# Bucketed attention and a GELU layer on one core: the first batch's softmax division moved behind the value product

## The chip, the core and the metric

One core of a Trainium2 chip. The metric is the device time of one execution in microseconds, lower is better; the median of several executions is compared. TensorE (PE) multiplies and also turns tiles; VectorE (DVE), ScalarE (ACT) and GpSimd (POOL) work element by element; SyncE (SP) issues the transfers.

## What is computed

```python
mask = q_bucket[:, :, :, None] == k_bucket[:, :, None, :]
scores = scale * np.matmul(q, k.transpose(0, 1, 3, 2))
scores = np.where(mask, scores, -1000000000.0)
scores = scores - np.max(scores, axis=-1, keepdims=True)
attn = np.exp(scores)
attn = attn / (np.sum(attn, axis=-1, keepdims=True) + 1e-09)
attn_out = np.matmul(attn, v)
x = attn_out.transpose(0, 2, 1, 3).reshape(B * S, H * D)
h = x @ w_in
out = 0.5 * h * (1.0 + erf(h / np.sqrt(2.0))) @ w_out
```

There are 4 batches, 8 heads, 768 positions and 64 features of a head; the bucket of a position is a number of 6 signs of a projection; the layer is 512 wide with 2048 hidden features. All inputs are float32.

## The kernel before

The work of the attention comes in units: one head and 128 queries against all 768 keys, 48 units in a batch, 192 in all. Two heads make a pair; 256 queries are a chunk, so a pair and a chunk take four units. For a unit (`unit`, L750), PE makes the scores with four matmuls (L765, ring `s` of 2 PSUM buffers), DVE finds the largest of each row (L768) and a small product of it (L772), ACT takes the exponentials into ring `p` (L778; 2 buffers in the first batch, a third later) and sums each row on the way. The sum gets 1e-9 added (`total`, on ACT, DVE or POOL) and DVE takes its reciprocal (L787).

From there the batches differ (`WHOLE`, L26). In batch 0 everything stays in float32: `whole_turn` (L824) multiplies the exponentials by the reciprocal in place (`divided`: 128x768 on ACT, DVE or POOL), PE turns them in six 128x128 transposes (L833) into two PSUM buffers of the ring `hp`, and two copies (ACT or DVE) bring them into the ring `pt`. `values` (L865) multiplies the turned tiles of a pair and chunk with the values (L880, 24 matmul records), and two steps bring the result into `x` in two float16 parts: ACT writes the high part with the scale of the values (L907), DVE the low part (L914). In the batches 1 to 3 the exponentials are divided and split into two float16 parts and turned by DMA; the change leaves these as they are.

Beside the units of batch 0 the same engines make the operands of each head (`head`: rounding, low parts, moves by an engine or by a DMA of SP, three projection matmuls, signs) and decode and split the weights (`weight_pair`, above all DVE: L486, L491, L496, L529, L555). The layer (L1074, ACT's gelu, L1122, L1141) follows chunk by chunk. Its first group of hidden features waits for the last score matmuls of batch 0 (`early_steps`), because its buffers lie where the fourth set of head operands lay.

All steps are listed first, each with engines it may run on, an estimated cost, a due time (the unit's number less or plus one of the numbers of `PAR`) and the steps it needs. `Plan.order` plays them through once, picks for each free engine the ready step that is due first, and so fixes the engine of each step and the order of each queue. On the chip every engine then works through its queue in that order; an instruction that waits holds everything queued behind it on its engine.

Of the kernel before, what the change touches and what calls it, by code (L numbers as in the profile page):

```python
# [32 lines left out]
PAR = dict(DR_ACT=180.03, DR_DVE=32.78, SI0=-234.76, SI1=321.18, SI2=-274.91, SI_ACT=-435.45, SI_DVE=-244.85, SI_Pool=-136.99, Z=598.64, VS0=-117.63, H0=565.92, HL=-600, VS=-594.8, G2=600, HQ=446.27, VQ=519.55, in0=341.87, out0=361.65, in1=54.07, out1=512.39, in2=153.92, out2=299.76, in3=338.81, out3=348.44, H1=487.41, H2=501.77, H3=-314.52, H4=53.2, H5=190.41, H6=-565.9, H7=135.72, MEV=-462.42, MGE=592.79, MSP=572.47, V0=-392.16, QK0=142.58, QK1=-179.17, QK2=174.11, MX0=-38.24, MX1=-334.15, MX2=-600, EX0=59.88, EX1=-101.95, EX2=460.15, NR0=94.12, NR1=-587.27, NR2=19.84, HI0=374.58, HI1=-275.4, HI2=-597.26, LO0=-600, LO1=-438.84, LO2=388.37, PV0=159.29, PV1=-533.03, PV2=-322.05, TR0=-526.38, TR1=-567.47, TR2=-42.11, V1=463.52, V2=314.42, Sin0=-61.75, Sin1=512.25, Sin2=326.03, Sin3=-253.09, Sout0=383.99, Sout1=-516, Sout2=360.56, Sout3=-232.19, Lin=532.76, Pin=460.34, Qin=600, Cin=-7.38, Min=536.23, Lout=600, Pout=600, Qout=-207.73, Cout=-600, Mout=363.48, G0=167.04, G1=-500.44, G3=146.24, G4=-508.01, G5=-323.28, G6=-126.53, G7=117.72, DUP0=357.52, DUP1=339.32, DUP2=361.88, LOW0=171.54, LOW1=-375.7, LOW2=-591.9, PRJ0=351.84, PRJ1=115.77, PRJ2=594.01, MSK0=404.11, MSK1=383.24, MSK2=187.87, DI_ACT=581.05, DI_DVE=-600, DI_Pool=587.5, WS_ACT=344.23, WS_DVE=401.15, WS_Pool=582.63, WH_ACT=-449.61, WH_DVE=519.61, WH_Pool=151.81, WL_ACT=-261.43, WL_DVE=-196.91, WL_Pool=-597.4, VH_ACT=345.12, VH_DVE=363.9, VH_Pool=-55.33, MV_SP=600, MV_ACT=600, MV_DVE=-499.53, MV_Pool=-197.62, LO_ACT=-128.53, LO_DVE=-14.71, LO_Pool=376.22, RND_ACT=-445.94, RND_DVE=62.58, RND_Pool=405.55, MSK_ACT=-183.07, MSK_DVE=-71.72, MSK_Pool=177.11, HI_ACT=96.96, HI_DVE=423.53, HI_Pool=32.64, DG_ACT=-156.41, DG_DVE=-190.46, DG_Pool=-42.95, EV_ACT=324.28, EV_DVE=41.66, EV_Pool=565.57, GH_ACT=50.45, GH_DVE=14.78, GH_Pool=91.5)  # L33
HOPX = {"PE": -0.03, "DVE": -0.1, "ACT": 0.12, "Pool": 0.27, "SP": 1.04}
BIG = 2.0**34
# [187 lines left out]
def tile_bucket_attention_moe(  # L223
# [33 lines left out]
        "s": 2, "hp": 4, "p": 2, "hl": 2, "raw": 1, "rawe": RAWE, "sign": 1, "pt": NTH + 1,  # L257
        "x": NTH, "vraw": 1, "vhl": 2, "wraw": 3, "o": 2, "diag": 1, "h": 1,
    }
# [3 lines left out]
    def ring(pool, name, shape, dtype, count, first=0):  # L263
# [16 lines left out]
        "vhl": ring(const, "vhl", [P, 2, KT, P], F16, 2),  # L280
        "wraw": [wbits[:, n * 1024 : (n + 1) * 1024] for n in range(rings["wraw"])],
        "o": ring(const, "o", [P, 1024], F32, rings["o"]),
        "diag": ring(const, "diag", [P, P], BF16, 1),
# [3 lines left out]
        for i in range(NSET)  # L287
    ]
    rows = const.tile([P, NT, 5], F32, tag="rows", name="rows")
    tiny = const.tile([P, 4 * NSC + 2 * B, 4], F32, tag="tiny", name="tiny")  # L290
# [15 lines left out]
    for i in range(NSET + 1, NSET + 1 + NEARLY):  # L306
        sets.append([
            early.tile([P, S], F32R, tag=f"{nm}{i}", name=f"{nm}{i}") for nm in ("Aq", "Ak", "Bq", "Bk")
        ])
    bufs["rawe"] = ring(early, "rawe", [P, S], F32, rings["rawe"])  # L310

# [438 lines left out]
    def unit(t, i, qs, cl, whole, made, place):  # L750
# [26 lines left out]
        def exps():  # L777
            nc.scalar.activation(  # L778
                out=buf(ex).rearrange("p (b k) -> p b k", b=2), in_=both(sp), func=AF.Exp, scale=sc, bias=nb,
                accum_out=ssum,  # L780
            )

        def total():
            affine(su.engine, si, ssum, unity, 1e-9 * unity)

# [18 lines left out]

        unity = 1.0 if whole else 2.0**-15
# [7 lines left out]
        if whole:  # L813
            return sp, whole_turn(ex, nr, r, place, cl, t)
        hi = add(affine_on("HI", S, True), 0, high, t + PAR[f"HI{cl}"], [nr], takes="hl", port=True)
# [5 lines left out]
        free(hi, [tr])  # L821
        return sp, [tr]

    def whole_turn(ex, nr, r, place, cl, t):  # L824

        hold, u = place

        def divided():
            affine(dg.engine, buf(ex), buf(ex), r)
# [13 lines left out]

        dg = add(affine_on("DG", S, True), 0, divided, t + PAR[f"HI{cl}"], [nr], port=True)
        if not hold:
            hold.append(add("none", 0, lambda: None, -10, [dg], takes="pt"))
        prods, copies = [], []
        for n, (k0, k1) in enumerate(((0, KT // 2), (KT // 2, KT))):
            step = []
            step.append(  # L850
                add("PE", TURN * (k1 - k0), lambda k0=k0, k1=k1, step=step: product(k0, k1, step), t + PAR[f"LO{cl}"], [dg, hold[0]], takes="hp")
            )
# [12 lines left out]
    def values(b, pr, ch, whole, vhl, turns, holds, key):  # L865

# [39 lines left out]
        def high():  # L906
            nc.scalar.activation(  # L907
                out=buf(xt[b, ch])[:, 0, pr, :nt], in_=buf(parts[0])[:, :nt], func=AF.Copy,
                scale=s_v[:, b : b + 1] if whole else 2.0**-15,
            )  # L910

        def low():
            x = buf(xt[b, ch])
            nc.vector.scalar_tensor_tensor(  # L914
                out=x[:, 1, pr, :nt], in0=buf(parts[0])[:, :nt], scalar=s_v[:, b : b + 1] if whole else 2.0**-15, in1=x[:, 0, pr, :nt],
                op0=ALU.mult, op1=ALU.subtract,
            )

        needs = [parts[-1]]
# [39 lines left out]
    for b in range(B):  # L959
# [3 lines left out]
        for h in range(2 * NPAIR):  # L963
            pr = h // 2
            if h % 2 == 0:
                key, mms = t - PAR[f"V{cl}"], []
                whole = pr < WHOLE[b]
                vhl = values_whole(b, pr, key) if whole else values_halves(b, pr, key, v_ready[b])
                holds, turns = {}, {}
            i = min(range(n_sets), key=lambda i: (used.get(i, -1), i))  # L970
# [4 lines left out]
            for ch in chunks:  # L975
                holds[h % 2, ch], turns[h % 2, ch] = [], []
                for u in range(ch[1] // P):
                    qs = slice(ch[0] + u * P, ch[0] + (u + 1) * P)
                    sp, tr = unit(t, i, qs, cl, whole, made, (holds[h % 2, ch], u))
                    uses.append(sp)  # L980
                    turns[h % 2, ch] += tr
                    t += 1
                if h % 2:
                    mms.append(
                        values(
                            b, pr, ch, whole, vhl, turns[0, ch] + turns[1, ch], [holds[0, ch], holds[1, ch]],
                            t + PAR[f"PV{cl}"],
                        )
                    )
# [238 lines left out]
```

## Time and profile before

| | |
|---|---|
| time, median of 3 runs | 901.4 us (901.18 to 901.84) |
| the profiled execution | 900.17 us, its span 898.1 us |
| PE, DVE, ACT, POOL busy | 95%, 77%, 71%, 25% of the span |
| granted TensorE clock, mean | 0.992 of full speed |

The span runs from the first to the last instruction of the profiled execution; its time has some 2 us around it. A busy time is the time in which at least one record of the engine is open. Records of one engine overlap: an instruction's record opens before the one ahead of it has closed, so what an instruction takes from its queue is the distance from its start to the next start, which is less than the length of its record. The same holds for matmuls more strongly.

### The profile page before, as it was taken

What the parts mean: (1) busy time and instruction counts of PE and PEld (TensorE: products, weight loads), DVE (VectorE), ACT (ScalarE), POOL (GpSimd) and SP (SyncE); (2) the same over time, 40 slices, a digit from 0 to 9 for tenths busy, and PEclk for the clock granted to TensorE, in tenths of its full rate; (3) what the DMA queues carried; (4) which work ended last, traced back from release to release, by engine and by line L of the source; (5) the groups of instructions that cost most, each with busy time, mean ns of one, the idle gap of its engine ahead of it and who ended that gap; (6) DMA issues with size and microseconds to landing.
All of it is one profiled execution on the core that took longest, in us unless ns stands there. A gap on an engine that the chain in (4) does not pass through costs nothing.

```text
span 898.1 us, 17035 instructions
## 1 busy us (share of the span) xinstructions
PE 855.6 (95%) x6452; PEld 610.5 (68%) x6452; DVE 695.3 (77%) x1337; ACT 635.0 (71%) x1050; POOL 225.8 (25%) x239
## 2 busy tenths in 40 slices
PE   4898988979999999999999999999999999999997
PEld 2665666766676777867677667767767767676663
DVE  8899999989999999987997987897897761212112
ACT  5888988786878878877787887887887762232231
POOL 5544534231422422310311323131231110000000
PEclk9899999989999999999999999999999999999999
DMA  8655542454496998875767689779499651000000
GB/s 269 189 180 168 147 133 95 112 124 94 107 161 145 208 211 161 172 152 117 163 150 158 153 165 188 137 143 189 80 195 145 118 111 20 24 1 25 1 24 23
DMA packets 269745, 115.79 MB, mean 129 GB/s; under 512 B 228576, under 2 KB 253152, under 8 KB 269664
## 3 DMA queue, kind: packets, MB, share of 16 engines
q1 hardware_dynamic: 269488, 114.72, 58.5%
q8 instruction: 50, 0.82, 0.4%
q14 instruction: 31, 0.25, 0.1%
q10 hardware_dynamic: 176, 0.00, 0.0%
HBM read 41.95 MB, written 6.29 MB: 54 GB/s over the span
## 4 chain that ended last, share of the span: by engine, by line
PE 75%; DVE 16%; ACT 5%; issue 2%; DMA 1%; SPq 0%; POOL 0%; DVEq 0%; ACTq 0%
PE hp L1141 25%; PE hp L1074 24%; PE s L765 12%; PE hp L889 8%; DVE s L768 4%; ACT p L778 2%; PE hp L880 1%; PE hp L833 1%; DVE Bq L688 1%; PE hp L725 1%; PE hp L727 1%; DVE hl L793 1%; DMA Bk<-Aq 1%; PE hp L726 1%; DVE wbits L793 1%
## 5 line engine op out<-in xcount | busy, mean ns | idle before, releaser
L1074 PE MATMUL hp<-x,Win 128*128 128x256 f16 x2304 | 267.5, 273 | 0.8 <-DVE tiny L529 0.8
L1141 PE MATMUL hp<-Wout,g 128*128 128x512 f16 x1152 | 265.6, 380 | 0.0
L1074 PEld LDWEIGHTS <-Win 128*128 128x128 f16 x2304 | 220.7, 98 | 41.2 <-issue 12.3
L1141 PEld LDWEIGHTS <-g 128*128 128x128 f16 x1152 | 107.1, 98 | 128.4 <-issue 13.3
L768 DVE TENSOR_REDUCE s<-s 128x1 f32<-128x768 f32 x192 | 181.7, 959 | 16.1 <-PE s L765 14.1
L778 ACT ACTIVATE p<-s,rows 128x768 f32<-128x768 f32 x148 | 145.9, 987 | 21.9 <-DVE rows L772 14.1
L765 PE MATMUL s<-Ak,Aq 128*128 128x384 f32 x360 | 141.7, 394 | 11.4 <-ACT p L778 9.5
L1084 ACT ACTIVATE h<-hp,ffs 128x512 f32<-128x512 f32 x96 | 65.2, 683 | 103.3 <-PE hp L1074 102.7
L765 PE MATMUL s<-Bk,Bq 128*128 128x384 f32 x360 | 123.3, 343 | 0.0
L1122 DVE SCALAR_TENSOR_TENSOR g<-h,ffs,g 128x512 f16<-128x512 f32 x96 | 75.2, 796 | 48.2 <-ACT g L394 43.4
L765 PEld LDWEIGHTS s<-Ak,Aq 128*128 128x128 f32 x360 | 69.2, 192 | 36.4 <-ACT p L778 23.1
L397 DVE TENSOR_SCALAR g<-h,ffs 128x512 f16<-128x512 f32 x42 | 21.2, 505 | 75.1 <-PE hp L1141 60.6
L889 PE MATMUL hp<-pt,vhl 128*64 128x256 f16 x1296 | 76.3, 274 | 1.7 <-DVE vhl L650 1.6
L889 PEld LDWEIGHTS <-vhl 128*64 128x64 f16 x1296 | 68.7, 110 | 11.1 <-issue 9.2
L765 PEld LDWEIGHTS s<-Bk,Bq 128*128 128x128 f32 x360 | 69.6, 193 | 1.0
L793 DVE SCALAR_TENSOR_TENSOR wbits<-p,rows,wbits 128x768 f16<-128x768 f32 x56 | 60.0, 1074 | 2.4 <-ACT wbits L394 2.1
L397 POOL TENSOR_SCALAR rows<-rows 128x1 f32<-128x1 f32 x50 | 20.0, 401 | 162.0 <-ACT p L778 89.6
L417 POOL TENSOR_TENSOR Bk<-raw,Aq 64x768 fp32r<-64x768 f32 x24 | 45.6, 1900 | 36.6 <-ACT Aq L394 35.2
L833 PE MATMUL hp<-ident,p 128*128 128x128 f32 x288 | 42.6, 282 | 8.1 <-POOL p L397 2.7
L778 ACT ACTIVATE wbits<-s,rows 128x768 f32<-128x768 f32 x44 | 43.3, 984 | 8.5 <-DVE rows L772 7.1
L793 DVE SCALAR_TENSOR_TENSOR hl<-p,rows,hl 128x768 f16<-128x768 f32 x44 | 45.9, 1051 | 1.0 <-POOL hl L397 0.7
L1108 ACT ACTIVATE h<-h 128x2048 f32<-128x2048 f32 x24 | 45.9, 1911 | 0.4
(164 smaller groups left out, 1167.5 us busy)
## 6 DMA issues: line engine op xcount, KB each, us to landing
raw<-qk SPq DMA_DIRECT2D x28, 384.0 KB, 3.6
vraw<-v SPq DMA_DIRECT2D x28, 384.0 KB, 4.0
wbits<-w_in SPq DMA_DIRECT2D x16, 512.0 KB, 3.7
wbits<-w_out SPq DMA_DIRECT2D x16, 512.0 KB, 4.2
out<-o SPq DMA_DIRECT2D x12, 512.0 KB, 2.8
Bq<-Aq SPq DMA_DIRECT2D x18, 192.0 KB, 2.8
Ak<-Aq SPq DMA_DIRECT2D x17, 192.0 KB, 3.0
Bk<-Aq SPq DMA_DIRECT2D x13, 192.0 KB, 2.9
```

Source lines behind the costliest of these rows:

```text
L417: on.tensor_tensor(out=out, in0=in0, in1=in1, op=ALU.subtract)
L765: nc.tensor.matmul(to, x, y, start=k == 0, stop=k == 1)
L768: nc.vector.tensor_reduce(out=buf(sp)[:, SPARE + 1 : SPARE + 2], in_=both(sp), axis=AX.XY, op=ALU.max, negate=True)
L778: nc.scalar.activation(out=buf(ex).rearrange("p (b k) -> p b k", b=2), in_=both(sp), func=AF.Exp, scale=sc, bias=nb, accum_out=ssum,)
L793: nc.vector.scalar_tensor_tensor(out=buf(hi)[:, 1], in0=buf(ex), scalar=r, in1=buf(hi)[:, 0], op0=ALU.mult, op1=ALU.subtract,)
L833: nc.tensor.transpose(buf(step[0])[:, (k - k0) * P : (k - k0 + 1) * P], buf(ex)[:, words(k)], ident32,)
L889: nc.tensor.matmul(pv[j * D : (j + 1) * D], buf(vh)[:, tv, kt, j * D : (j + 1) * D], buf(holds[j][0])[:, tp * KT + kt, :nt], start=kt == 0 ...
L1074: nc.tensor.matmul(buf(pair[0])[:, j * ch[1] : (j + 1) * ch[1]], win_hl[:, f0 // WB1, tw, pr, f0 % WB1 : f0 % WB1 + P], x[:, tx, pr, : ch[1]],
L1084: nc.scalar.activation(out=bufs["h"][0][:, 2 * fp : 2 * fp + 2, :nt], in_=buf(pair[0])[:, : 2 * nt].rearrange("p (j k) -> p j k", j=2), fu ...
L1108: nc.scalar.activation(out=h, in_=h, func=AF.Gelu)
L1122: nc.vector.scalar_tensor_tensor(out=gt[:, 1, s2, :nt], in0=h[:, s2, :nt], scalar=sg, in1=gt[:, 0, s2, :nt], op0=ALU.mult, op1=ALU.subtract,)
L1141: nc.tensor.matmul(buf(banks[u]), gt[:, tg, f, u * P : (u + 1) * P], wout_hl[:, ft // UT, tw, ft % UT], start=fresh and f == ti == 0, stop ...
```

## The change

In batch 0 the exponentials are no longer divided before they are turned. `whole_turn` needs only the exponentials. Their row sums go to a column each of a new tile `sums`. For each pair and chunk (12 in the batch) a new function `divisors` works on the sums of its four units at once: it adds 1e-9, takes one reciprocal of 128x4, spreads the factors to a tile of 128x256 (each factor 64 times), lets PE turn this with two 128x128 transposes into a buffer of `hp`, and copies it to SBUF (`rb`, 2 buffers). After the value product, DVE multiplies the product by the scale of the values and by these factors (`divided`, in `values`) into `rb`, an engine writes the high float16 part from it and DVE or POOL subtracts for the low part; before, ACT and DVE did the two parts straight from PSUM. The two transposes of `divisors` join `early_steps`, so the layer's first group waits for them too. All due times are other numbers, the planner's estimate of a transpose is 0.11 in place of 0.1 and three of its hop times are others, so the whole order is made anew, that of the later batches too.

```diff
-TURN = 0.1
+TURN = 0.11
...
-HOPX = {"PE": -0.03, "DVE": -0.1, "ACT": 0.12, "Pool": 0.27, "SP": 1.04}
+HOPX = {"PE": -0.03, "DVE": -0.09, "ACT": 0.12, "Pool": 0.01, "SP": 0.82}
...
-                accum_out=ssum,
+                accum_out=sums[:, t : t + 1] if whole else ssum,
...
+        if whole:
+            return sp, whole_turn(ex, place, cl, t), ex
...
-        dg = add(affine_on("DG", S, True), 0, divided, t + PAR[f"HI{cl}"], [nr], port=True)
         if not hold:
-            hold.append(add("none", 0, lambda: None, -10, [dg], takes="pt"))
+            hold.append(add("none", 0, lambda: None, -10, [ex], takes="pt"))
...
+    def divisors(t, cl, exs):
...
+        def spread():
+            for_u = all_of(shares).rearrange("p j u -> p u j").unsqueeze(3)
+            affine(rs.engine, buf(rs), for_u.to_broadcast([P, UT, 2, D]))
+
+        def turn():
+            for u in range(UT):
+                nc.tensor.transpose(
+                    buf(rt)[:, u * P : (u + 1) * P], buf(rs)[:, u].rearrange("p j d -> p (j d)"), ident32
+                )
+
+        def copy():
+            affine(rc.engine, buf(rc), buf(rt)[:, :TC])
+
+        su = add({e: (c, PAR[f"SI_{e}"]) for e, c in (("ACT", 0.23), ("DVE", 0.07), ("Pool", 0.16))}, 0, total, t + PAR["RB"], exs)
+        nr = add("DVE", 0.07, norm, t + PAR["RB"], [su])
+        rs = add(affine_on("RS", TC), 0, spread, t + PAR["RB"], [nr], takes="spread", port=True)
+        rt = add("PE", 2 * TURN, turn, t + PAR["RB"], [rs], takes="hp")
+        free(rs, [rt])
+        early_steps.append(rt)
+        rc = add({e: (c, PAR[f"EV_{e}"]) for e, c in (("ACT", 0.28), ("DVE", 0.34))}, 0, copy, t + PAR["RB"], [rt], takes="rb")
+        free(rt, [rc])
+        return rc
...
+        def divided():
+            nc.vector.scalar_tensor_tensor(
+                out=buf(rc), in0=buf(parts[0])[:, :nt], scalar=s_v[:, b : b + 1], in1=buf(rc),
+                op0=ALU.mult, op1=ALU.mult,
+            )
...
         if whole:
-            needs.append(v_ready[b])
-        hi = add("ACT", 0.06 + 0.21 * nt / TC + 0.093 * whole, high, -10, needs)
-        lo = add("DVE", 0.07 + 0.27 * nt / TC, low, -10, [hi])
-        free(parts[0], [lo])
+            xm = add("DVE", 0.41, divided, -10, [parts[-1], rc, v_ready[b]])
+            free(parts[0], [xm])
+            hi = add(affine_on("XH", TC), 0, high_of, -10, [xm], port=True)
+            lo = add(subtract_on("XL", TC), 0, low_of, -10, [hi], port=True)
+            free(rc, [lo])
```

## Rows read from the trace of the kernel before

**Rows 1.** Windows: stretch, length; PE, PEld, DVE, ACT, POOL busy (records); clock; DMA.

```profile
22.00:166.00 144.00, 129.21 (x905) 92.17 (x906) 138.99 (x322) 125.83 (x253) 65.72 (x69) 0.98 0.51 147
166.00:202.00 36.00, 31.39 (x237) 25.13 (x236) 33.68 (x63) 29.01 (x46) 10.05 (x10) 0.91 0.58 131
202.00:898.00 696.00, 685.59 (x5276) 487.20 (x5274) 503.68 (x924) 468.37 (x736) 137.42 (x141) 1.00 0.60 121
```

**Rows 2.** The same view, two pieces of the first stage.

```profile
22.00:90.00 68.00, 59.33 (x397) 42.12 (x398) 64.66 (x150) 59.06 (x116) 33.16 (x35) 0.96 0.61 180
90.00:108.00 18.00, 17.96 (x123) 12.40 (x122) 17.80 (x43) 16.32 (x36) 8.83 (x9) 1.00 0.40 121
```

**Rows 3.** Chain that ended last, 88:108 (start us, us, what).

```profile
93.18 0.90 PE s L765 x4
94.08 0.66 PE hp L833 x6
94.73 1.01 PE hp L880 x8
...
101.76 0.71 PE s L765 x4
```

**Rows 4.** Lines on PE, 22:166 (count | busy us, mean ns | idle before).

```profile
L833 PE MATMUL hp<-ident,p 128*128 128x128 f32 x284 | 42.1, 282 | 8.1 <-POOL p L397 2.7 <-DVE x L914 1.9 <-DVE rows L772 1.2
```

**Rows 5.** The same view, DVE.

```profile
L768 DVE TENSOR_REDUCE s<-s 128x1 f32<-128x768 f32 x46 | 43.9, 957 | 3.2 <-PE s L765 3.1
L397 DVE TENSOR_SCALAR pt<-hp 128x384 f32<-128x384 f32 x29 | 15.8, 551 | 0.9 <-PE hp L833 0.7
...
L787 DVE RECIPROCAL rows<-rows 128x1 f32<-128x1 f32 x47 | 7.4, 158 | 0.2
...
L914 DVE SCALAR_TENSOR_TENSOR x<-hp,s_v,x 128x256 f16<-128x256 f32 x11 | 5.2, 477 | 0.0
...
L397 DVE TENSOR_SCALAR p<-p,rows 128x768 f32<-128x768 f32 x2 | 1.2, 622 | 0.0
```

**Rows 6.** The same view, ACT.

```profile
L394 ACT ACTIVATE pt<-hp 128x384 f32<-128x384 f32 x65 | 29.6, 486 | 6.8 <-PE hp L833 6.3
L394 ACT ACTIVATE p<-p,rows 128x768 f32<-128x768 f32 x25 | 23.2, 935 | 5.8 <-DVE rows L787 5.6
...
L394 ACT ACTIVATE rows<-rows 128x1 f32<-128x1 f32 x27 | 5.5, 202 | 0.7
L907 ACT ACTIVATE x<-hp,s_v 128x256 f16<-128x256 f32 x11 | 5.1, 465 | 1.5 <-PE hp L880 1.4
```

**Rows 7.** The same view, POOL.

```profile
L397 POOL TENSOR_SCALAR p<-p,rows 128x768 f32<-128x768 f32 x21 | 21.0, 1001 | 38.1 <-DVE rows L787 29.3 <-DVE rows L772 2.6 <-DVE tiny L387 2.5
L417 POOL TENSOR_TENSOR Bk<-raw,Aq 64x768 fp32r<-64x768 f32 x4 | 8.1, 2026 | 5.7 <-ACT Aq L394 5.4
...
L397 POOL TENSOR_SCALAR diag<-ident,tiny 128x128 bf16<-128x128 bf16 x4 | 1.5, 373 | 4.3 <-DVE tiny L529 1.9 <-PE hp L432 0.9 <-DVE inv_v L383 0.9
```

**Rows 8.** DVE, then ACT in order of time (start us, us, instruction).

```profile
71.60 0.16 DVE L787 RECIPROCAL rows<-rows 128x1 f32<-128x1 f32 x1
71.67 0.21 DVE L772 SCALAR_TENSOR_TENSOR rows<-limit,s 128x2 f32<-128x2 f32 x1
...
73.80 0.20 ACT L394 ACTIVATE rows<-rows 128x1 f32<-128x1 f32 x1
73.91 0.47 ACT L394 ACTIVATE pt<-hp 128x384 f32<-128x384 f32 x1
74.28 0.39 ACT L394 ACTIVATE diag<-ident,tiny 128x128 bf16<-128x128 bf16 x1
```

**Rows 9.** What PE waited for, 22:166 (us in total, times, longest us).

```profile
PE hp L833 <- POOL p L397: 2.7, 3, 1.2
```

**Rows 10.** PE, then ACT in order of time, the end of the first batch.

```profile
159.84 1.47 PE L1074 MATMUL hp<-x,Win 128*128 128x256 f16 x12
...
160.71 0.99 ACT L778 ACTIVATE p<-s,rows 128x768 f32<-128x768 f32 x1
```

More of the change, by code (lines that the diff above doesn't have):

```diff
@@ L257, in tile_bucket_attention_moe @@
         "s": 2, "hp": 4, "p": 2, "hl": 2, "raw": 1, "rawe": RAWE, "sign": 1, "pt": NTH + 1,
-        "x": NTH, "vraw": 1, "vhl": 2, "wraw": 3, "o": 2, "diag": 1, "h": 1,
+        "x": NTH, "vraw": 1, "vhl": 2, "wraw": 3, "o": 2, "rb": 2, "spread": 1, "diag": 1, "h": 1,
     }
@@ L288, in tile_bucket_attention_moe @@
     ]
+    n_whole = 2 * KT * WHOLE[0]
+    assert not any(WHOLE[1:])
+    sums = const.tile([P, n_whole + KT], F32, tag="sums", name="sums")
+    shares = const.tile([P, n_whole + KT], F32, tag="shares", name="shares")
     rows = const.tile([P, NT, 5], F32, tag="rows", name="rows")
@@ L309, in tile_bucket_attention_moe @@
         ])
+    bufs["spread"] = ring(early, "spread", [P, UT, 2, D], F32, 1)
     bufs["rawe"] = ring(early, "rawe", [P, S], F32, rings["rawe"])
@@ L821, in unit, with whole_turn @@
         free(hi, [tr])
-        return sp, [tr]
-    def whole_turn(ex, nr, r, place, cl, t):
+        return sp, [tr], ex
+    def whole_turn(ex, place, cl, t):
         hold, u = place
-        def divided():
-            affine(dg.engine, buf(ex), buf(ex), r)
         def product(k0, k1, step):
@@ L850, in whole_turn @@
             step.append(
-                add("PE", TURN * (k1 - k0), lambda k0=k0, k1=k1, step=step: product(k0, k1, step), t + PAR[f"LO{cl}"], [dg, hold[0]], takes="hp")
+                add("PE", TURN * (k1 - k0), lambda k0=k0, k1=k1, step=step: product(k0, k1, step), t + PAR[f"LO{cl}"], [ex, hold[0]], takes="hp")
             )
@@ L863, in whole_turn, with all_of, total, norm @@
         return copies
-    def values(b, pr, ch, whole, vhl, turns, holds, key):
+    def divisors(t, cl, exs):
+        def all_of(tile_):
+            return tile_[:, t : t + 2 * KT].rearrange("p (j k) -> p j k", j=2)[:, :, : UT]
+        def total():
+            affine(su.engine, all_of(sums), all_of(sums), 1.0, 1e-9)
+        def norm():
+            nc.vector.reciprocal(out=all_of(shares), in_=all_of(sums))
+        def spread():
[17 more added lines that the diff above has]
+        return rc
+    def values(b, pr, ch, whole, vhl, turns, holds, key, rc):
         vh, vl = vhl
@@ L907, in high @@
             nc.scalar.activation(
-                out=buf(xt[b, ch])[:, 0, pr, :nt], in_=buf(parts[0])[:, :nt], func=AF.Copy,
-                scale=s_v[:, b : b + 1] if whole else 2.0**-15,
+                out=buf(xt[b, ch])[:, 0, pr, :nt], in_=buf(parts[0])[:, :nt], func=AF.Copy, scale=2.0**-15,
             )
@@ L914, in low, with high_of, low_of @@
             nc.vector.scalar_tensor_tensor(
-                out=x[:, 1, pr, :nt], in0=buf(parts[0])[:, :nt], scalar=s_v[:, b : b + 1] if whole else 2.0**-15, in1=x[:, 0, pr, :nt],
+                out=x[:, 1, pr, :nt], in0=buf(parts[0])[:, :nt], scalar=2.0**-15, in1=x[:, 0, pr, :nt],
                 op0=ALU.mult, op1=ALU.subtract,
             )
-        needs = [parts[-1]]
-        if whole:
-            needs.append(v_ready[b])
-        hi = add("ACT", 0.06 + 0.21 * nt / TC + 0.093 * whole, high, -10, needs)
-        lo = add("DVE", 0.07 + 0.27 * nt / TC, low, -10, [hi])
-        free(parts[0], [lo])
+        def divided():
[3 more added lines that the diff above has]
+            )
+        def high_of():
+            affine(hi.engine, buf(xt[b, ch])[:, 0, pr, :nt], buf(rc))
+        def low_of():
+            x = buf(xt[b, ch])
+            subtract(lo.engine, x[:, 1, pr, :nt], buf(rc), x[:, 0, pr, :nt])
+        if whole:
+            xm = add("DVE", 0.41, divided, -10, [parts[-1], rc, v_ready[b]])
[3 more added lines that the diff above has]
+            free(rc, [lo])
+        else:
+            hi = add("ACT", 0.06 + 0.21 * nt / TC, high, -10, parts[-1:])
+            lo = add("DVE", 0.07 + 0.27 * nt / TC, low, -10, [hi])
+            free(parts[0], [lo])
         x_parts[b, ch] += [hi, lo]
@@ L968, in tile_bucket_attention_moe @@
                 vhl = values_whole(b, pr, key) if whole else values_halves(b, pr, key, v_ready[b])
-                holds, turns = {}, {}
+                holds, turns, exs = {}, {}, []
             i = min(range(n_sets), key=lambda i: (used.get(i, -1), i))
@@ L978, in tile_bucket_attention_moe @@
                     qs = slice(ch[0] + u * P, ch[0] + (u + 1) * P)
-                    sp, tr = unit(t, i, qs, cl, whole, made, (holds[h % 2, ch], u))
+                    sp, tr, ex = unit(t, i, qs, cl, whole, made, (holds[h % 2, ch], u))
                     uses.append(sp)
+                    exs.append(ex)
                     turns[h % 2, ch] += tr
@@ L983, in tile_bucket_attention_moe @@
                 if h % 2:
+                    rc = divisors(t - KT - UT, cl, exs[-KT - UT : -KT] + exs[-UT:]) if whole else None
                     mms.append(
```

10 lines of the change are left out of this document (4 added, 6 removed).

## Prediction

> **What bounds the kernel now.** I read the windows first, to see which engine is full in which stretch. From 202 us on, PE has records open in 685.6 of 696 us at full clock [rows 1]: there the end moves only with PE's work, and the change takes none from it. What can be won lies before. In the stage of the first batch, 22 to 166 us, DVE is open in 139.0 of 144 us (96.5%), ACT in 125.8 (87%), PE in 129.2 and POOL in 65.7 [rows 1]. So DVE is the fullest, with ACT near behind, and the pieces say the same: 64.7 of 68 us up to 90, then 17.8 of 18 [rows 2].
>
> A busy PE is not a full one, so I read the chain next, in the one piece where it runs through PE alone: four score matmuls take 0.71 to 0.90 us, six transposes 0.66, eight matmuls of the value product 1.01 [rows 3]. A unit has four, six and six of these: 0.71 + 0.66 + 0.76 = 2.1 us at the least and 2.3 at the most. The stage holds 46 units [rows 5], 98 to 107 us. They are 184 + 284 + 264 of PE's 905 records (the last: 11 products of 24, as there are 11 of L914) [rows 1, 4, 5]; for the other 173 I estimate 0.11 each as of a transpose, 19 us. PE thus has 117 to 126 us of work in 144. It is the third engine near its limit, but in this stage not the first. The stage ends when the last of three queues is through, and shortening it shortens the whole, since what follows is PE's own work in an unbroken row.
>
> **What an instruction takes from its queue.** Records overlap. On DVE a reciprocal of 0.16 us is followed after 0.07, so 0.09 is hidden; on ACT a small step of 0.20 is followed after 0.11 and a copy of 0.47 after 0.37, so 0.10 is [rows 8]. I take 0.09 and 0.10 off the mean lengths below.
>
> **Removed and added, DVE.** 47 reciprocals of 0.07 (3.3 us) become 12 of much the same length (0.8): 2.5 less. Two divisions of 128x768 go, 2 x 0.53 = 1.1 [rows 5]. Sure: 3.6 us. The new product with the factors stands in for the low part from PSUM (0.477 [rows 5]), same size, one PSUM and one SBUF operand; I take no difference, bounded by the overlap at 12 x 0.09 = 1.1 us either way. The new low part costs 12 x 0.39 = 4.7 us if DVE does it, by the same row, and nothing if POOL does.
>
> **ACT.** 25 divisions of 0.935 go (20.9 us), 27 of the steps that add 1e-9 (2.7), 11 high parts from PSUM of 0.465 (4.0) [rows 6]: 27.6 us less. Back come, if ACT takes them, 12 copies of the turned factors and 12 high parts, both priced by the same 128x256 row at 0.37: 8.8 us. From below, a high part on DVE could be a third of a 128x768 division there, 0.21 [rows 5]; from above, a copy on DVE the 0.46 of a 128x384 one. I take the ACT row, which has the same size.
>
> **POOL.** 21 divisions (21.0 us) go [rows 7]. It was no bound and stays none, with 12 spreads of the factors: between 0.21 (a third of the DVE row) and 0.47 (the ACT row of that size), 0.37 by POOL's 128x128 step; and 12 low parts, between 0.68 (a third of its 128x768-wide subtraction of 2.03) and 2.03 [rows 7]. I take 0.37 and 0.68: 12.6 us.
>
> **What moves with it.** ACT ends some 19 us emptier, DVE only 4. The order is planned anew, and the steps that may go to either are the copies of the turned exponentials, 29 on DVE at 0.46 = 13.4 us [rows 5], 0.39 each on ACT = 11.3 [rows 6]. If all go over, DVE stands at 139.0 - 3.6 - 13.4 = 122.0 and ACT at 125.8 - 27.6 + 8.8 + 11.3 = 118.3. At most 17.0 us come off the fullest queue; with none moved and the low parts and factor copies on DVE it is 3.6 - 4.7 - 5.5, 6.6 us more than now.
>
> **PE.** 24 more transposes at 0.11 [rows 3], 2.6 us. I cost them at nothing: PE has 14.8 us with no record open in the stage [rows 1]. With that cover gone they cost 2.6. The trace has a mean record of 282 ns for one transpose [rows 4], and six of them in 0.66 us [rows 3]; the second is what the queue pays. The Trainium skill (TensorE: Matmul & The Clock Gate, Part 4: PE-mode transpose) gives about 275 ns for one in a kernel's context, which speaks against putting more of them on PE: by it 24 would cost 6.6 us, and the case of a small gain below would end at 905.1, slower than before. The record's length agrees with it, its spacing does not.
>
> **Waits.** The exponentials go to PE without sum, reciprocal and division between, over 1.2 us shorter; PE waited 2.7 us for POOL's divisions alone [rows 9], and the two buffers of `p` come free earlier. New is PE's wait for the spread factors: behind it in PE's queue stand the scores of the next units, and DVE and ACT wait for those. After the last exponentials of a set it is a sum (0.20), a reciprocal (0.16), a spread (0.37) and hand-overs, about 1 us, 1.1 with these estimated. The product with the factors also holds DVE's queue if the copy is late. At the end, the layer's first group, at 159.8 now, before the last exponentials of the batch are through (start 160.7, 0.99 long) [rows 10], must wait for the last turned factors, to about 162.8. Twelve matmuls, 1.5 us of filling, come later; transposes that no longer wait for a division can take their place. Between 0 and 1.5, I take half, 0.7.
>
> **The sum.** After the change three queues hold 122 (DVE), 118 (ACT) and 120 to 128 us (PE, with the 2.6). Such tightness occurs: from 90 to 108 us DVE was open in 17.8, ACT in 16.3 and PE in all of 18 us [rows 2]. Over a whole stage no row shows it; from 22 to 90, DVE lost 3.3 us though PE was less full. So I take about half of the 17.0: 9 us. The profiled execution of 900.2 us (span 898.1 and 2.1 around it) becomes 900.2 - 9 + 0.7 = 891.9. The median of the runs shown is 1.2 above it: 893.1.
>
> **Rivals.** *Nearly all comes through* (13 to 17 us): for it speaks that POOL's 26 us of removed work also lets it take operand steps from the other two, against it PE's 120 to 128. With 17.0: 885.1. *Only the sure part* (0 to 5 us): PE was the real limit, or the copies stay. With 3.6: 901.4 - 3.6 + 0.7 = 898.5, and 901.1, no change, if PE's 2.6 lie open too. *Slower: the turned factors hold PE.* Twelve times the queue stops at the factor transposes for the chain of 1.1 us, 13.2 us in all, because the order puts them right behind their exponentials. Against the 8.3 won that is 4.9 more: 906.3. It decides from a mean wait of 0.7 us per set, 8.3 / 12. For it: queues are strictly in order, and the hand-over times in the planner changed. Against it: nothing needs the factors before the value product is done, so they can stand late in the queue.
>
> **Chances.** Forecast, 5 to 13 us won (889 to 897): 0.45. Nearly all: 0.17. Small or none (897 to 903): 0.18, half of it within 0.2%, about what a measurement of this kernel can tell from no change (1.8 us, 899.6 to 903.2). Slower: 0.20. So faster 0.71, same 0.09, slower 0.20. The range goes from 884, the nearly-all case with a gate that costs nothing, to 905, which leaves out the worse half of the slower case.
>
> **What would show it.** In the stage of the first batch of the changed kernel: no division of `p`, 12 reciprocals where 47 were; most copies into `pt` on ACT; DVE some 15 us less busy; the stage some 9 us shorter, and the time after it as now. Wrong would be: waits of PE at the factor transposes of over 0.7 us each (the slower case), DVE's copies unmoved (the small one), or the stage shorter and the stretch after 202 us longer, if the new order gave back there what it won.

## The result and the profile after

The changed kernel takes 887.2 us (885.7 to 888.3), the kernel before on the same chip 901.3 us (900.7 to 901.8): a ratio of 0.9843, interval 0.9826 to 0.9860. It is 14.1 us faster where 8.3 were forecast; the time lies in the range, between the forecast and the case in which nearly all comes through. The profiled execution has a span of 883.9 us, 14.2 less than before.

To compare the stages I cut both traces where the last transposes of the first batch's exponentials start (166.4 us before, 155.0 after) and where the layer's first long run of matmuls starts (173.5 and 164.2). The windows of before and of after; the columns are PE, PEld, DVE, ACT and POOL busy, each with its number of records, the granted clock, the DMA share and GB/s. Before:

```profile
22.00:166.40 144.40, 129.61 (x908) 92.50 (x909) 139.39 (x324) 126.23 (x253) 66.12 (x69) 0.98 0.51 148
166.40:173.50 7.10, 7.10 (x61) 5.34 (x60) 7.10 (x18) 6.41 (x12) 0.28 (x1) 1.00 0.35 97
173.50:898.10 724.60, 709.48 (x5450) 506.65 (x5447) 529.86 (x967) 490.57 (x770) 146.79 (x150) 1.00 0.60 121
```

After:

```profile
22.00:155.00 133.00, 121.35 (x901) 92.92 (x900) 131.12 (x286) 108.86 (x223) 38.89 (x40) 0.99 0.53 159
155.00:164.20 9.20, 9.02 (x68) 5.67 (x67) 9.20 (x21) 6.57 (x15) 1.76 (x2) 1.00 0.45 117
164.20:883.90 719.70, 707.82 (x5469) 508.75 (x5467) 531.05 (x971) 472.56 (x753) 173.61 (x161) 1.00 0.61 123
```

The first batch's stage is 11.4 us shorter. The mark is not all of the first batch: the changed kernel has 48 matmul records of value products left behind it, the kernel before 24, which in turn had run 12 of the layer's matmuls ahead of it. DVE is still the full engine: 131.1 of 133.0 us (98.6%) after 139.4 of 144.4 (96.5%). Its records are open 8.3 us less there, and it stands idle 3.1 us less. ACT, from which the change took most, went from 87% to 82%. The stretch behind gains 4.9 us from the second cut, or 2.8 counted from the first.

What DVE no longer does in the stage, and what it does instead. First groups of DVE before (lines view, 22 to 166 us) that the rows ahead of the prediction do not show:

```profile
...
L555 DVE SCALAR_TENSOR_TENSOR Win<-Wout,tiny,Win 128x1024 f16<-128x1024 f32 x2 | 3.4, 1702 | 0.0
L555 DVE SCALAR_TENSOR_TENSOR Win<-Win,tiny 128x1024 f16<-128x1024 f32 x2 | 3.3, 1674 | 0.0
L555 DVE SCALAR_TENSOR_TENSOR Wout<-Win,tiny,Wout 128x1024 f16<-128x1024 f32 x2 | 2.6, 1279 | 0.0
L555 DVE SCALAR_TENSOR_TENSOR Wout<-Wout,tiny 128x1024 f16<-128x1024 f32 x2 | 2.5, 1273 | 0.0
...
L417 DVE TENSOR_TENSOR Bk<-raw,Aq 64x768 fp32r<-64x768 f32 x1 | 1.3, 1332 | 0.0
```

The same view of DVE after, 22 to 155 us:

```profile
...
L403 DVE TENSOR_SCALAR pt<-hp 128x384 f32<-128x384 f32 x34 | 18.2, 551 | 0.9 <-PE hp L835 0.7
...
L954 DVE SCALAR_TENSOR_TENSOR rb<-hp,s_v,rb 128x256 f32<-128x256 f32 x10 | 4.7, 472 | 0.0
...
L561 DVE SCALAR_TENSOR_TENSOR Win<-Win,tiny 128x1024 f16<-128x1024 f32 x2 | 2.5, 1274 | 0.0
L875 DVE RECIPROCAL shares<-sums 128x4 f32<-128x4 f32 x12 | 2.0, 170 | 0.0
...
L403 DVE TENSOR_SCALAR rb<-hp 128x256 f32<-128x256 f32 x4 | 1.7, 414 | 0.0
L561 DVE SCALAR_TENSOR_TENSOR Win<-Wout,tiny,Win 128x1024 f16<-128x1024 f32 x1 | 1.3, 1274 | 0.0
...
L423 DVE TENSOR_TENSOR x<-rb,x 128x256 f16<-128x256 f32 x1 | 0.4, 418 | 0.0
```

Four things stand here. The 47 reciprocals of [rows 5] are 12 (7.4 us of records to 2.0), and the divisions are gone. The low parts of the weights, eight before (L555, 11.8 us), are three (L561, 3.8 us): the other five have moved behind the stage, where PE is the fullest engine; what they cost there no run shows. DVE does not have fewer copies of turned exponentials but more: 34 where [rows 5] has 29. And some of its instructions are shorter, though nothing in them was changed. Two of the low parts of before were 2.1 us long, where the others take 1.28 (so the means of 1.70 and 1.67 above); a POOL record was open as each of the two began. One of them, in the timelines of DVE and of POOL before (start us, us):

```profile
83.62 2.07 DVE L555 SCALAR_TENSOR_TENSOR Win<-Win,tiny 128x1024 f16<-128x1024 f32 x1
...
83.05 1.56 POOL L397 TENSOR_SCALAR Win<-Wout,tiny 128x1024 f16<-128x1024 f32 x1
```

Four DVE records of this stage before are 0.5 to 0.9 us longer than the median of their kind, 2.8 us in all; after, none is more than 0.2 longer. Over the profiles of all runs here there are 64 DVE records, up to the stage end, that are over 0.25 us longer than their kind, and beside each of the 64 a POOL record is open, though POOL is busy in only 46% of the stage before. So emptying POOL gave DVE time too, most likely; which operation of POOL's holds up which of DVE's was not tried. ACT after, in the same view and window:

```profile
...
L400 ACT ACTIVATE pt<-hp 128x384 f32<-128x384 f32 x61 | 27.1, 485 | 3.0 <-PE hp L835 2.8
...
L400 ACT ACTIVATE spread<-shares 128x256 f32<-128x256 f32 x10 | 4.2, 416 | 4.4 <-DVE shares L875 4.3
...
L400 ACT ACTIVATE x<-rb 128x256 f16<-128x256 f32 x7 | 2.9, 415 | 5.0 <-DVE rb L954 5.0
L400 ACT ACTIVATE rb<-hp 128x256 f32<-128x256 f32 x7 | 2.7, 383 | 0.5 <-PE hp L883 0.5
```

And POOL after:

```profile
L423 POOL TENSOR_TENSOR Bk<-raw,Aq 64x768 fp32r<-64x768 f32 x5 | 9.1, 1828 | 2.1 <-ACT Aq L400 1.7
L423 POOL TENSOR_TENSOR x<-rb,x 128x256 f16<-128x256 f32 x9 | 7.0, 777 | 27.2 <-ACT x L400 19.1 <-DVE x L403 7.8
```

POOL, free of the divisions, makes five low parts of head operands of this form where [rows 7] has four (the one that DVE made, L417 of before, is gone there) and all but one of the new low parts. ACT's share of the copies into `pt` is 61 where [rows 6] has 65.

How far PE runs behind its own work shows where the time was won. For each kernel I gave each matmul the spacing that it has in an unbroken row in these traces (0.109 us for a hidden-layer matmul or a transpose, 0.216 for an output one, 0.174 for a score, 0.126 and 0.054 for a value product in the first and the later batches), which makes, as an estimate, 814.2 us of work before and 816.8 after (24 transposes more), and compared the start times with the work done so far (us):

```
PE's work done   behind, before   behind, after   won since the line above
130              48.5             38.5            10.0
180              59.7             46.4             3.3
400              67.0             55.2            -1.5
all              79.0             62.4             4.8
```

That is 16.6 us, less the 2.6 of new transposes 14.0. Ten fall into the first batch, three into the turn to the layer; 1.5 are lost again up to 400 us of work, and near five are won behind that, in a stretch that the change touches by nothing but its order.

### The profile page after: what moved, and what is told of

It reads as the page before. It is cut to its first block, busy times and chain, and to the rows that moved or that the text cites. A ratio compares the mean times of both kernels' runs of the same rounds, so it can differ in the third digit from the quotient of the medians.

```text
span 883.9 us, 16956 instructions
## 1 busy us (share of the span) xinstructions
PE 848.5 (96%) x6476; PEld 614.3 (69%) x6476; DVE 689.8 (78%) x1303; ACT 600.6 (68%) x1008; POOL 228.9 (26%) x223
## 4 chain that ended last, share of the span: by engine, by line
PE 74%; DVE 17%; ACT 5%; issue 2%; DMA 1%; POOL 0%; SPq 0%; DVEq 0%; ACTq 0%
PE hp L1127 26%; PE hp L1194 25%; PE s L771 11%; PE hp L924 7%; DVE s L774 5%; DVE pt L403 1%; ACT p L784 1%; PE hp L731 1%; DVE Bq L694 1%; DVE Wout L497 1%; DVE rows L778 1%; PE hp L733 1%; PE hp L732 1%; DVE Wout L502 1%; PE hp L835 1%
## 5 line engine op out<-in xcount | busy, mean ns | idle before, releaser
L774 DVE TENSOR_REDUCE s<-s 128x1 f32<-128x768 f32 x192 | 180.2, 958 | 10.6 <-PE s L771 8.2
L771 PE MATMUL s<-Ak,Aq 128*128 128x384 f32 x360 | 138.8, 385 | 11.5 <-ACT p L784 9.4
L1175 DVE SCALAR_TENSOR_TENSOR g<-h,ffs,g 128x512 f16<-128x512 f32 x96 | 78.1, 830 | 57.6 <-ACT g L400 53.8
L403 DVE TENSOR_SCALAR g<-h,ffs 128x512 f16<-128x512 f32 x34 | 18.5, 548 | 72.9 <-PE hp L1194 63.5
L423 POOL TENSOR_TENSOR Bk<-raw,Aq 64x768 fp32r<-64x768 f32 x28 | 53.9, 1923 | 42.3 <-ACT Aq L400 41.2
L799 DVE SCALAR_TENSOR_TENSOR wbits<-p,rows,wbits 128x768 f16<-128x768 f32 x50 | 52.0, 1042 | 2.2 <-ACT wbits L400 1.0
L799 DVE SCALAR_TENSOR_TENSOR hl<-p,rows,hl 128x768 f16<-128x768 f32 x50 | 51.6, 1039 | 2.1 <-ACT hl L400 1.0
L403 POOL TENSOR_SCALAR rows<-rows 128x1 f32<-128x1 f32 x36 | 16.6, 460 | 91.3 <-ACT p L784 63.0
```

What stands on the lines that cost most here:

```text
L423: on.tensor_tensor(out=out, in0=in0, in1=in1, op=ALU.subtract)
L771: nc.tensor.matmul(to, x, y, start=k == 0, stop=k == 1)
L774: nc.vector.tensor_reduce(out=buf(sp)[:, SPARE + 1 : SPARE + 2], in_=both(sp), axis=AX.XY, op=ALU.max, negate=True)
L799: nc.vector.scalar_tensor_tensor(out=buf(hi)[:, 1], in0=buf(ex), scalar=r, in1=buf(hi)[:, 0], op0=ALU.mult, op1=ALU.subtract,)
L1175: nc.vector.scalar_tensor_tensor(out=gt[:, 1, s2, :nt], in0=h[:, s2, :nt], scalar=sg, in1=gt[:, 0, s2, :nt], op0=ALU.mult, op1=ALU.subtract,)
```

## The experiments

Times are medians, each with its ratio to the kernel before on the same chip and the interval. "Stage end" is the start of the last transpose of the first batch's exponentials in the profile of each run.

| run | time, us | ratio to before | stage end, us |
|---|---|---|---|
| before | 901.3 | | 166.4 |
| changed | 887.2 | 0.9843 (0.9826 to 0.9860) | 155.0 |
| new structure, old numbers | 915.7 | 1.0148 (1.0122 to 1.0174) | 164.4 |
| old structure, new numbers | 944.3 | 1.0474 (1.0459 to 1.0490) | 214.4 |
| before, division aside | 901.7 | 1.0007 (0.9997 to 1.0017) | 165.0 |
| before, division left out | 899.4 | 0.9985 (0.9973 to 0.9997) | 166.6 |
| before, sums and reciprocals out too | 896.9 | 0.9969 (0.9953 to 0.9985) | 163.8 |
| changed, factors turned without a wait | 887.3 | 0.9847 (0.9813 to 0.9881) | 156.3 |
| changed, division put back | 909.7 | 1.0101 (1.0062 to 1.0139) | 179.4 |
| changed, more on DVE | 911.5 | 1.0107 (1.0065 to 1.0149) | 180.2 |
| changed, more on ACT | 889.6 | 0.9871 (0.9837 to 0.9905) | 159.2 |
| changed, a third of DVE's copies moved | 888.7 | 0.9877 (0.9848 to 0.9905) | 157.0 |
| changed, copies planned on ACT alone | 919.8 | 1.0221 (1.0190 to 1.0252) | 178.9 |
| changed, old late numbers | 930.3 | 1.0338 (1.0305 to 1.0371) | 155.9 |

The theory is that of the prediction: DVE with ACT bounds the first batch, and the work taken off them carries the gain. The rivals: the new order carries it, or the wait for the division did.

### Structure and order, one without the other

```diff
--- the changed kernel, with the numbers of before
-TURN = 0.11
+TURN = 0.1
-PAR = dict(DR_ACT=-582.95, ...)
+PAR = dict(DR_ACT=180.03, ..., RB=-170.85, RS_ACT=-216.44, ...)
-HOPX = {"PE": -0.03, "DVE": -0.09, "ACT": 0.12, "Pool": 0.01, "SP": 0.82}
+HOPX = {"PE": -0.03, "DVE": -0.1, "ACT": 0.12, "Pool": 0.27, "SP": 1.04}
```

> The changed kernel with the planner's numbers of before (due times, transpose estimate, hop times; only the due times of the new steps are the new ones). If the work taken off the engines carries the gain, most of the 7.1 us that PE's queue gained in the first batch stays: 892 to 897. If the new numbers carry it, little is left: 899 to 906.

915.7 us, 1.5% slower than before and outside both of the ranges expected. In the profiled execution (911.7 us, the fastest of the four) the stage is 2.0 us shorter (164.4), so less work helped a little, but what follows takes 745.5 us where before it took 731.7. The windows of this run, cut at its own stage end:

```profile
22.00:164.40 142.40, 126.44 (x912) 94.28 (x911) 136.10 (x289) 106.74 (x220) 43.45 (x43) 0.98 0.52 152
164.40:909.90 745.50, 723.55 (x5534) 515.02 (x5532) 545.92 (x999) 490.93 (x764) 161.87 (x157) 0.99 0.59 120
```

DVE is busy 136.1 of 142.4 us: its share is lower than in either kernel, 95.6%. ACT's freed room (106.7 of 142.4) is not used.

```diff
--- the kernel before, with the numbers of the changed one (the DG ones its own)
-PAR = dict(DR_ACT=180.03, ...)
+PAR = dict(DR_ACT=-582.95, ..., DG_ACT=-156.41, DG_DVE=-190.46, DG_Pool=-42.95)
...
```

> The kernel before with the new numbers (due times, transpose estimate, hop times; those of the division step as before). If the work taken off carries the gain: no gain, 899 to 912, as numbers made for another structure can only fit worse. If the new numbers carry it: 889 to 896. If they carry only what was won after the first batch (PE's queue gained some 5 us after 400 us of its work): 896 to 899.

944.3 us, 4.7% slower and beyond all three ranges. Neither half is faster; both together are. A set of due times belongs to one structure, and the gain can't be shared out between the two by taking one away: these two runs say what a wrong order costs, not what a right one brings.

### The division, with the order of before held still

With the order untouched, load and wait can be told apart. The three runs here leave the division out of the result. In the first, `aside` is a float16 tile that nobody reads; a buffer of `p` still comes free only when the division has read it.

```diff
         def divided():
-            affine(dg.engine, buf(ex), buf(ex), r)
+            affine(dg.engine, aside[dg.engine], buf(ex), r)
```

> The kernel before, its order untouched: the 48 divisions of the first batch are computed as before but into a tile that nobody reads, and the undivided exponentials are turned (so the division is missing from the result). The engines' work stays, PE's wait for sum, reciprocal and division goes. If the waits were the price: 894 to 897. If the work was: 899.5 to 901.5.

901.7 us, ratio 1.0007: taking PE's wait for the division away alone brings nothing. PE's transposes stand in its queue where the old order put them, and PE waits elsewhere: for score buffers that ACT must empty, 9.8 us up to the stage end, where it was 5.3 in the kernel before.

```diff
         def divided():
-            affine(dg.engine, buf(ex), buf(ex), r)
+            pass
```

> The kernel before, its order untouched, the 48 divisions of the first batch left out (missing from the result). Work and wait go. Against the run with the division aside it shows the work alone. Either theory: 890 to 896; if the work is the price, 5 us or more below the run with the division aside; if the wait is, within 2 us of it. Well below 890 would say that the new steps behind the value product cost the change a good part of its gain.

899.4 us, ratio 0.9985: 48 instructions of 0.6 to 1 us left out, 46 of them on ACT and POOL, bring 1.4 us (0.3 to 2.4), less than any theory had. At this order neither engine is the one that the stage waits for.

```diff
         def total():
-            affine(su.engine, si, ssum, unity, 1e-9 * unity)
+            if not whole:
+                affine(su.engine, si, ssum, unity, 1e-9 * unity)
 
         def norm():
-            nc.vector.reciprocal(out=r, in_=si)
+            if not whole:
+                nc.vector.reciprocal(out=r, in_=si)
```

> The kernel before, its order untouched, without the divisions of the first batch and now without their sums and reciprocals too (the division is missing from the result). Against the run that leaves out the divisions alone (899.4) DVE's queue is 48 x 0.07 + 7 x 0.07 = 3.9 us shorter. If DVE bounds the first batch whatever the order: 895 to 896.5. If what it frees is lost in other waits of an order made for longer steps: 897.5 to 900.

896.9 us, ratio 0.9969, 2.8 us below the kernel before. Against the run above that is 1.4 us more by the ratios, whose intervals overlap, and 2.8 us at the stage end (163.8 against 166.6), of an estimated 3.9 taken off DVE. The run takes 40 small sums off ACT and POOL besides. These small steps weigh as much as the 48 large ones, but at a fixed order not all of what DVE is spared comes through.

So leaving the whole division out at the old order is worth 2.8 us; the changed kernel, which has all its new steps besides, gains 14.1. The rest, some 11 us, appears only with an order made for the new steps. Whether another order made for the old steps would have brought part of it is not shown.

### More work, with the new order held still

```diff
+            if whole:
+                for _ in range(3):
+                    nc.vector.reciprocal(out=idle[:, :1], in_=limit[:, :1])
```

> The changed kernel, its order untouched, with three reciprocals of 128x1 more on DVE in each of the 48 units of the first batch, written to a place nobody reads: 48 x 3 x 0.07 = 10 us of DVE's queue. If DVE bounds the first batch: 7 to 10 us more than the changed kernel, 894 to 897.5. If PE does: 0 to 4 more, 887 to 891.

911.5 us: 24 above the changed kernel by the ratios. The expectation had the price wrong. Three in a row take 0.47 us, as DVE's timeline in this run shows (60.80 to 61.27; start us, us):

```profile
60.69 0.19 DVE L779 SCALAR_TENSOR_TENSOR rows<-limit,s 128x2 f32<-128x2 f32 x1
60.80 0.56 DVE L785 RECIPROCAL idle<-limit 128x1 f32<-128x1 f32 x3
61.27 0.95 DVE L775 TENSOR_REDUCE s<-s 128x1 f32<-128x768 f32 x1
```

48 x 0.47 = 22.6 us more on DVE, 25.2 at the stage end, 24 in the time: in the changed kernel, work added to DVE in the first batch is paid in full.

```diff
+            if whole:
+                for _ in range(2):
+                    affine("ACT", idle[:, 1:], limit[:, 1:])
```

> The changed kernel, its order untouched, with two small copies of 128x1 more on ACT behind each unit's exponentials in the first batch: 48 x 2 x 0.11 = 10.6 us of ACT's queue. If ACT is loose there (busy 81% of the stage): 0 to 3 us more, 887 to 890. If it is as tight as DVE: 7 or more, 894 to 898.

889.6 us, 2.5 above the changed kernel by ratios whose intervals overlap; the stage ends 4.2 us later. Here too the price was too low: two take 0.34 us, 16.3 in all. ACT's timeline in this run:

```profile
72.31 0.20 ACT L785 ACTIVATION_READ_ACCUMULATOR p<-s,rows 128x1 f32 x1
72.40 0.43 ACT L401 ACTIVATE idle<-limit 128x1 f32<-128x1 f32 x2
72.74 0.98 ACT L785 ACTIVATE p<-s,rows 128x768 f32<-128x768 f32 x1
```

A microsecond more on ACT is thus worth 0.15 to 0.26 us, one on DVE 1.06 to 1.12. DVE bounds the stage of the changed kernel and ACT does not.

```diff
+            if whole:
+                affine(("ACT", "Pool")[t % 2], buf(ex), buf(ex), one1)
```

> The changed kernel, its order untouched, with a 128x768 multiplication by one in place behind each unit's exponentials in the first batch, on ACT and POOL in turn: the load of the old division and its wait ahead of the transposes, at an order that does not know of them. If the removed work is what the new order lives on: 13 us or more, 900 to 915 (24 more steps of 0.84 us on ACT are 20 us, of which its idle time in the stage, some 25 us, hides a part at best). If the removed work was of no account and the numbers only happen to be better: under 893.

909.7 us, 23 above the changed kernel, the stage end 24.4 us later. ACT has 24 steps more, some 21 us, against the 16.3 of the run above, which moved the stage end by 4.2. One difference is that PE's transposes now wait for the step. The windows of this run up to its stage end, and what PE waited for up to there:

```profile
22.00:179.30 157.30, 129.56 (x903) 93.63 (x903) 140.85 (x287) 130.96 (x249) 66.22 (x65) 0.97 0.45 137
```

```profile
PE hp L839 <- POOL p L405: 10.4, 12, 1.7
...
PE hp L839 <- ACT p L402: 1.7, 3, 1.1
```

DVE is busy 140.9 of 157.3 us, 89.5%: it waits 16.4 us where in the changed kernel it waited 1.9. PE waits 12.1 us for the steps put back, which the changed kernel does not have. So under the new order the short way from the exponentials to the transposes counts, while under the old one (division aside) PE's wait counted nothing. How much of the 23 us it is stays open. By the price of the run above ACT's 21 us of load are some 5, an estimate, and 15 DVE records are longer than their kind beside an open POOL record, 7.5 us in all. The three were not separated.

### The new steps

```diff
-                    buf(rt)[:, u * P : (u + 1) * P], buf(rs)[:, u].rearrange("p j d -> p (j d)"), ident32
+                    buf(rt)[:, u * P : (u + 1) * P], ident32, ident32
```

> The changed kernel, its order untouched: PE turns the constant identity in place of the spread factors, so the same 24 transposes wait for nothing (the division is then wrong in the first batch's result). If PE's queue is held by the factors (the slower rival of the prediction): 5 us or more below the changed kernel's 887.2, under 882. If the order has them late enough, as the trace says (PE waited 0.6 us in all ahead of them, and that for other buffers): 886 to 888.5.

887.3 us, ratio 0.9847: as the changed kernel. PE's queue is not held by the factors. The waits of PE in the changed kernel, 22 to 155 us, say the same (us in total, times, longest): ahead of the factor transposes it waited for nothing but free buffers.

```profile
PE s L771 <- ACT p L784: 5.0, 4, 2.8
PE hp L835 <- DVE rb L954: 1.5, 2, 1.1
...
PE hp L883 <- ACT pt L400: 0.6, 2, 0.4
```

The 2.7 us for POOL's divisions [rows 9] are gone. The 1.5 for the new product on DVE (L954), which holds a PSUM buffer, stand where 1.9 for the old low part (L914) were [rows 4].

### DVE's copies, the step that the prediction counted on

```diff
+            n_dve[0] += on == "DVE"
+            if on == "DVE" and n_dve[0] % 3 == 0:
+                on = "ACT"
```

> The changed kernel, its order untouched but for every third of DVE's copies of turned exponentials, which ACT does at the same place of the order: 12 x 0.47 = 5.6 us off DVE, 12 x 0.39 = 4.7 us onto ACT. By the runs with more work (1.07 us of time for one on DVE, 0.2 to 0.4 for one on ACT) 6.0 less and 1 to 2 more: 882 to 884. If ACT's place in the chain matters more than its load (exponentials behind such a copy come later, and DVE's next maximum waits for their buffer): 887 to 893.

888.7 us, ratio 0.9877 against 0.9843 of the changed kernel, and a stage end 2.0 us later. Eleven copies in the window (23 left of 34) went over, 5.2 us off DVE, and nothing was won. The window of this run up to its stage end:

```profile
22.00:157.00 135.00, 122.00 (x902) 93.69 (x903) 129.57 (x276) 113.35 (x237) 39.00 (x40) 0.99 0.51 158
```

DVE now stands idle 5.4 us, where in the changed kernel it was 1.9: it waits 1.0 us for scores (none in the changed kernel), 1.4 for transposes (0.7 there) and 0.9 for a step of ACT (0.3 there). What DVE was spared it lost in part to these waits.

```diff
-            done = add(
-                {e: (c, PAR[f"EV_{e}"]) for e, c in (("ACT", 0.38), ("DVE", 0.47))}, 0,
+            done = add(
+                {"ACT": (0.38, PAR["EV_ACT"])}, 0,
...
```

> The changed kernel planned anew with ACT as the only engine for the copies of the turned exponentials, as the prediction took them: 16 us off DVE in the first batch, 13 onto ACT. If the prediction's step holds, that DVE's copies are what the room on ACT is good for: 878 to 886. If ACT is then the full one (128 us of work up to the stage's end become 141 of 164) or the numbers don't fit the plan: 889 to 905.

919.8 us, 2.2% slower than before and beyond both ranges. What PE waited for in this run, against 9.4 us for the same releaser in the changed kernel's whole span:

```profile
PE s L771 <- ACT p L784: 24.2, 17, 6.1
...
PE hp L835 <- ACT p L784: 3.7, 4, 2.2
```

Scores wait for a buffer that the exponentials must empty, and these stand behind copies on ACT; DVE's next maximum waits for the scores. That reads as if ACT were loose by its load and tight by its place. But this run can't show it, for it was planned anew and DVE is full again. Its window up to the stage end, and in it the low parts of the weights:

```profile
22.00:178.90 156.90, 129.85 (x916) 96.75 (x917) 148.71 (x289) 121.16 (x256) 50.23 (x45) 0.95 0.48 143
```

```profile
L561 DVE SCALAR_TENSOR_TENSOR Win<-Win,tiny 128x1024 f16<-128x1024 f32 x4 | 5.1, 1276 | 0.0
L561 DVE SCALAR_TENSOR_TENSOR Win<-Wout,tiny,Win 128x1024 f16<-128x1024 f32 x4 | 5.1, 1276 | 0.0
L561 DVE SCALAR_TENSOR_TENSOR Wout<-Wout,tiny 128x1024 f16<-128x1024 f32 x4 | 5.0, 1275 | 0.0
...
L561 DVE SCALAR_TENSOR_TENSOR Wout<-Win,tiny,Wout 128x1024 f16<-128x1024 f32 x2 | 2.5, 1257 | 0.0
```

DVE is busy 148.7 of 156.9 us, without a single copy of turned exponentials: all 14 low parts of the weights are in this stage, where the changed kernel has three, and 13 records are longer than their kind beside an open POOL record, some 9 us in all. So the 34 us by which this run is slower than the changed kernel can be in good part DVE's other work, which this plan does earlier. What the copies on ACT cost by themselves was not separated.

### The later batches

```diff
--- the changed kernel; the attention's numbers that end in 1 or 2 as before (QK1, MX1, EX1, ..., PV2, TR2)
-PAR = dict(..., QK1=63.5, QK2=20.7, MX1=-7.86, ...)
+PAR = dict(..., QK1=-179.17, QK2=174.11, MX1=-334.15, ...)
```

> The changed kernel with the attention's due times of before for the batches 1 to 3 (those of the first batch, of weights and of engines stay new). If the 3 to 5 us that PE's queue gained after 400 us of its work are the new due times of the later batches: 890 to 894, with the first batch as in the changed kernel. If they follow from a first batch that ends earlier: 886 to 889. A mixture that fits nothing would show as more than 895.

930.3 us, with the first batch as in the changed kernel (stage end 155.9 against 155.0). The mixture fits nothing. PE falls back in two stretches:

```profile
200.00:400.00 200.00, 192.17 (x1490) 135.99 (x1489) 181.41 (x335) 146.89 (x232) 57.70 (x53) 0.99 0.74 151
400.00:700.00 300.00, 300.00 (x2357) 215.95 (x2356) 230.82 (x423) 207.35 (x326) 73.68 (x76) 1.00 0.67 135
700.00:927.80 227.80, 202.21 (x1392) 138.14 (x1389) 95.61 (x170) 99.27 (x151) 12.46 (x12) 0.94 0.28 58
```

From 700 us on PE is open in only 202.2 of 227.8 us, and the granted clock is 0.94 where the changed kernel has 1.00 from 700 us on. The due times of the later batches thus decide over tens of microseconds by themselves. That the five won there come from them is likely by the size of this effect, but not shown: the first batch that ends earlier and the weights' work that now stands behind it are rivals, and with these numbers no run that fits could tell them apart.

## Why the prediction was right, and where not

*What bounds the kernel.* Right, and shown for the changed kernel: a microsecond more on DVE in the first batch costs a microsecond, one on ACT a quarter or less, and the factors' wait on PE nothing. For the kernel before the support is weaker: of an estimated 3.9 us spared on DVE 2.8 came through at the stage end and 1.4 in the time.

*DVE, the sure part.* Right: reciprocals 12 for 47, divisions gone, the new product as long as the old low part (472 ns for the 477 of [rows 5]). The new low parts went to POOL but for one, the value I took.

*ACT and POOL.* Of the spreads, which I gave to POOL, ten went to ACT and one to POOL in the stage. POOL's new low parts took 0.78 us each where I had 0.68, a third of a row that I read as 128x768 wide; it is 64x768 [rows 7]. Neither mattered, as neither engine is the bound. What I had at nothing is that DVE's records lengthen beside open POOL records: 2.8 us before, none after.

*What moves with it.* Wrong. I gave ACT's room to DVE's copies, 13.4 of the 17.0 us. The plan left them on DVE (34 for 29). By my own sign (copies unmoved) the small case should have come, and it did not. The failed step is pricing a move by the load of the two engines alone: with the order held, eleven copies moved spared DVE 5.2 us and won nothing (888.7 against 887.2 us), and DVE stood idle 3.5 us more. That a step on ACT ahead of exponentials delays what feeds DVE is my reading of this. It is not shown, and the small steps added on ACT, which stood there too, cost only a quarter of their length or less. In place of the copies DVE lost other work: five low parts of weights, 8.0 us of records (1.6 of them the stretched part of two), moved behind the stage, and one low part of a head's operands is gone from it. That this work of the weights can wait is nowhere in my sum.

*The sum.* "About half of 17.0" came to 9; DVE's busy time in the stage shrank by 8.3, where I had some 15, and its idle time by 3.1, so the stage by 11.4. The size is near by luck: my 9 was made of copies that never moved.

*PE.* The 2.6 us at nothing: on the way to 130 us of PE's work, ten were won and 2.6 spent, so the net of the first batch is 7.4. The new transposes waited 0.6 us in all. From the start of one to the next instruction's start they take 0.17 us in the mean, 4.1 us for the 24: within a pair the second follows after 0.11 to 0.17, not always after the 0.11 that I took. By the 275 ns of the Trainium skill (TensorE: Matmul & The Clock Gate, Part 4: PE-mode transpose), measured there with bf16, they would have taken 6.6, an estimate; the records of the new ones are that long (median 273 ns), their spacing is not.

*Waits and the gate.* The slower rival did not come: the factor transposes stand late enough. The gate did not decide either: the last factor transposes start at 156.4 us, the layer's first matmul at 164.0, for the new order puts other work ahead. In the kernel before 24 matmuls of the layer ran ahead of the long row; now none do, 2.6 us of filling given up where I had 0.7.

*After 202 us.* Wrong: "the end moves only with PE's work, and the change takes none from it". PE was open in 685.6 of 696 us [rows 1], but open is not working: before, it fell 12.0 us further behind its own work after 400 us of it, now 7.2. The row could not show that, and I had warned of it for the first stage only. This term, nought in my sum, is some 5 us, with 3 more at the turn to the layer and 1.5 lost between: 6.6 us, about all of what the change gained beyond the forecast (5.8).

*Order.* I wrote of the order as something that follows from the work. Under the old numbers the work saved is worth nothing: the same structure is 13 us slower than before. What stays open is how much a new set of numbers alone could bring to the old structure. The new set is no answer to it (4.7% slower), and a set made for that would be another search.

## What to carry to other kernels

A microsecond taken from an engine is worth what the order makes of it: leave the work out at the old order (here 2.8 us for the whole division) before counting on it, and put it back at the new one (23 us) to see what the new order lives on. Don't price a move between engines by the two loads alone: try it with the order held, and look where the relieved engine then waits. And look past the stage that a change is about: a planned order is remade everywhere, and a stretch whose busiest engine is 98% open can still have several microseconds in it.

## What the runs showed of the hardware that I had not expected

Small instructions have no fixed price. A reciprocal of 128x1 on DVE gave way to the next instruction after 0.07 us where other kinds followed it [rows 8], but three in a row that write the same place took 0.155 each in the mean: the first two gave way after 0.197 (median), which is after their own end, the third after 0.08. Small copies on ACT took 0.17 in such a row where a single step of this size had taken 0.11: the first gave way after 0.22, the second after 0.11. It goes with the shared target and not with the same kind: in the run with more on DVE a reciprocal that writes elsewhere starts 0.08 us after the third of such a row. The three take 0.47 us from the first's start to its start (timeline of DVE, start us, us):

```profile
62.72 0.55 DVE L785 RECIPROCAL idle<-limit 128x1 f32<-128x1 f32 x3
63.19 0.14 DVE L394 RECIPROCAL tiny<-inv 128x1 f32<-128x1 f32 x1
```
